# Stage-1 units one place later, and one matrix load behind a transposing transfer

## The chip, the cores and the metric

One of the eight cores of a Trainium2 chip runs the program. The metric is the device time of one execution in microseconds. The median of three runs of the kernel before is 1419.41 us (1419.1 to 1424.3). Times inside the program come from one further execution that the hardware profiler recorded; they count from the first instruction of its span.

## The reference

Block-causal attention, then a gated layer pair, then a mixture of experts with a greedy assignment of tokens:

```
scores = (q @ k^T) / sqrt(64); mask by blocks of 64; attn = softmax(scores)
x   = attn @ v                              # 8 batches x 8 heads x 576 x 64 -> 4608 x 512
x   = ((x @ w1) * (x @ w2)) @ w3 @ w_out     # 512 -> 1024 -> 1024 -> 512
logits = x @ w_gate                         # 8 experts
assign each token to an expert, pairs (token, expert) in falling order of logit, 576 tokens each
out[tokens of e] = relu(x @ ew1[e]) @ ew2[e]
```

Everything is kept exact enough by splitting operands into a high and a low half in a narrow type; a product is then three matmuls.

## The kernel before

**Stage 1** works in half steps h = 0 to 63, two for each pair of heads, eight for each batch b. A half step makes score tiles on TensorE (`s_tiles`, lines 331 to 395), their exponentials on ScalarE (357), sums, scaled high and low halves on VectorE and ScalarE (P, 371 to 377), a transposing DMA of P on SP's queue (416, `PT`), and some half steps later the product with v (`pv`, 434), whose result is read out by ScalarE (445) and VectorE (440) into `xT[b]`. `xT[b]` holds all 512 features of a batch's 576 tokens.

Between them run the **units** of `moe_unit`: 128 of them, 16 for each batch. Unit u takes half of a batch's tokens (288) and one of eight column blocks of w1 and w2: 12 matmuls for w1 and 12 for w2 (line 467), a read-out by ScalarE (`a_sb`, 477), the product on VectorE (`g`, 483), and, every second unit, a write of `g` to DRAM on SP's queue (485). The eight units of the first token half of batch b need four finished `pv` of that batch, those of the second half all eight. Smaller products follow the units: `logits` (521), and `turn` (542 to 546), which brings the routing logits into the tile `L` by way of ScalarE's copies `lgT` (529).

The order is a list of events by place: `at(p, f)` puts f at place p, counted in half steps, and events run in the order of p. On TensorE this order is binding in stage 1 (`manual_schedule` with PE alone); on the other engines a scheduler orders the instructions. The units' places are `slots`: two in each half step, at .26 and at .6. The units of batch 0 take the first 16 slots; from unit 16 on two slots are skipped. Events after h = 64 (units, logits, loads for the next stage) form a tail without attention work; it closes with `run(70.2)` and the logits of the last 16 units.

**Stage 2** routes: seven phases of short VectorE and TensorE steps that depend on one another. It starts from `L`. The waits of TensorE in it are filled with the matmuls `px` (1161), which compute the 36 blocks of 128 rows of x; each block is written to `xr` in DRAM by SP's queue (1218), the last one by SP (1212) for the 512 values and by ScalarE's queue (1214, `sq`) for a sum of squares for each row, 128 values of 4 bytes.

**Stage 3** computes the experts. `gather(p)` fetches 128 rows of `xr` at a time by an indirect DMA from GpSimd's queue (1340), splits them (`x16`, 1344 and 1345) and turns them: the first block on TensorE (1350, read out at 1353 and 1355 as `xT`), all others by a transposing DMA on SP's queue (1360). `layer1` (1387) and `layer2` (1405) follow. For the first expert, layer 1 runs over token blocks: eight products for the first 128 tokens, eight for the second, eight for the third, eight for the last 192, which reach over the fourth and fifth block. The experts' matrices are 2048 KB each and come by SP's queue (1249, `esa` and `esb`) into a buffer of one; `behind_row` puts such a load behind the transfer kept in `last_row[0]` in SP's order. The load of expert 2's first matrix is the first one that `phase_of` issues this way; its values are first read in the third of the calls of `phase_of`.

Of the kernel before, what the change touches and what calls it, by code (L numbers as in the profile page):

```python
# [56 lines left out]
def moe_kernel(ctx, tc, q, k, v, moe_w1, moe_w2, moe_w3, moe_w_out, w_gate, ew1, ew2, out):  # L57
    nc = tc.nc
    P = 128
# [16 lines left out]
    def pow2(pool, m, name, TB=TB, **kw):  # L76
        n = m.shape[-1]
        t = pool.tile([P, 3, n], I32, name=name, **kw)
        nc.vector.tensor_scalar(t[:, 0], m.bitcast(I32), 24, 23, op0=ALU.logical_shift_right,
                                op1=ALU.logical_shift_left)  # L80
        nc.vector.tensor_scalar(t[:, 1], t[:, 0], -1.0, float((189 + TB) << 23), op0=ALU.mult, op1=ALU.add)
        nc.vector.tensor_scalar(t[:, 2], t[:, 0], float((65 - TB) << 23), None, op0=ALU.add)
        return t[:, 1].bitcast(F32), t[:, 2].bitcast(F32)
# [33 lines left out]
    def at(p, f, *a):  # L117
        assert p >= now[0], (p, now[0])
        heapq.heappush(ev, (p, at.n, f, a))
        at.n += 1  # L120
# [6 lines left out]
    def run(end):  # L127
        while ev and ev[0][0] < end:
            now[0], _, f, a = heapq.heappop(ev)
            f(*a)  # L130
# [381 lines left out]
    def logits(u):  # L512
        b, r = divmod(u, 16)
        half, f = divmod(r, 8)
        if f == 0:
            hold("l")
            lg["ps"] = ps_ab.tile([P, 512], F32, name="ab")
        p = lg["ps"]
        gh = lg.pop(u) if u >= UL else lt[u // 8][:, u % 8]
        r = 32 * (f % 4)  # L520
        nc.tensor.matmul(p[r:r + 32, :288], W34g[:, f, :], gh, start=f < 4, stop=f >= 4)
        if f < 7:
            return
        odd = b % 2

        def rows_out():
            if half == 0:
                lgT[0] = mo.tile([P, S], F32, name="lgT", bufs=1)
            nc.scalar.activation(lgT[0][:, half * 288:half * 288 + 288], p[:, :288], AF.Copy)
            if half == 1 and not odd:  # L530
                lgT[1] = mo.tile([P, 64], F32, name="lgx", bufs=2)
                nc.scalar.activation(lgT[1], p[:, 224:288], AF.Copy)
            held.remove("l")
            if half == 1:
                defer(.1, alone, "l", turn)

        def turn():
            hold("l")
            t, n = lgT[0], 4 + odd
            p = ps_ab.tile([P, 512], F32, name="ab")  # L540
            if odd:
                nc.tensor.matmul(p[:64, :8], lgT[1], i8, start=True, stop=True)
                nc.tensor.matmul(p[64:, :8], t[:, :64], i8, start=True, stop=True)
            for j in range(odd, n):
                c = j * P - 64 * odd
                lg["o"] = nc.tensor.matmul(p[:, j * 8:j * 8 + 8], t[:, c:c + P], i8, start=True, stop=True)
            jb = 9 * (b // 2) + 4 * odd

            def keep():
                nc.vector.tensor_copy(L[:, jb:jb + n, :], p[:, :n * 8].rearrange("p (j e) -> p j e", e=8))  # L550
                held.remove("l")

            defer(.06, keep)

        defer(.1, rows_out)
# [229 lines left out]
    def pair(h):  # L785
        b, r = divmod(h, 8)
        return 4 * b + r % 4, int(r < 4)
# [17 lines left out]
        at(h, tiles, h)  # L805
    for h in range(2 * NS):
        at(h + 1.35 if h + 1 < HS else h + 2.93, alone, "v", pv, *pair(h))
    slots = [h + x for h in range(5, 73) for x in (.26, .6)]
    for u in range(128):
        at(slots[u if u < 16 else u + 2], moe_unit, u)  # L810
    for n in range(NS):
        b, r = divmod(n, 4)
        at(8 * b + r + (.85 if b < 2 else 1.7), prep_v, n)
# [365 lines left out]
    def prep_g(j, d=0):  # L1179
        load_g(j)  # L1180
        split_g(j, d)
# [42 lines left out]
    def fill(n):  # L1224
        owed[0] += n
        while owed[0] >= 1:
            owed[0] -= 1
            next(st_, None)
# [7 lines left out]
    early, last_row = {}, [None]  # L1236
# [47 lines left out]
    at(67.9, prep_g, 0, 1.0)  # L1284
    at(68.3, prep_g, 1, 1.0)
    with tc.manual_schedule(engines=MS):
        run(70.2)
        for u in range(UL, 126):
            logits(u)
            if u % 8 == 7:  # L1290
                run(now[0] + .5)
        fill(16)
        for u in range(126, 128):
            logits(u)
        run(100)
        prep_g(2)
# [34 lines left out]
    xT2, scs, hs, scat = {}, {}, {}, []  # L1331

    def gather(p):
        def block(h):
            if h == 0:
                xT2[p] = ce.tile([P, 8, NG * P], F16, name="xT2")
                scs[p] = ce.tile([P, NG], F32, name="sc")
            xg = ce.tile([P, DM + 1], F32, name="xg", bufs=4)
            c = p * NG + h
            nc.gpsimd.indirect_dma_start(out=xg, out_offset=None, in_=xr,  # L1340
                                         in_offset=bass.IndirectOffsetOnAxis(ap=idx[:, c:c + 1], axis=0))
            x16 = ce.tile([P, 2, DM], F16, name="x16", bufs=4)
            s, i = pow2(ce, xg[:, DM:], "xsc", TBX, bufs=4)
            nc.scalar.activation(x16[:, 0], xg[:, :DM], AF.Copy, scale=s)  # L1344
            nc.vector.scalar_tensor_tensor(x16[:, 1], xg[:, :DM], s, x16[:, 0], op0=ALU.mult, op1=ALU.subtract)  # L1345
            def by_pe():
                for z in range(2):
                    t = pe_.tile([P, 512], F32, name="pe")
                    for c_ in range(4):
                        nc.tensor.matmul(t[:, c_ * P:c_ * P + P], x16[:, z, c_ * P:c_ * P + P], id16, start=True, stop=True)  # L1350
                    dst, src_ = xT2[p][:, 4 * z:4 * z + 4, :P], t.rearrange("p (c t) -> p c t", c=4)
                    if z:
                        nc.vector.tensor_copy(dst, src_)
                    else:
                        nc.scalar.activation(dst, src_, AF.Copy)  # L1355

            if p == 0 and h == 0:
                owed_.append(by_pe)
            else:
                nc.sync.dma_start_transpose(out=xT2[p][:, :, h * P:h * P + P], in_=x16.rearrange("p z d -> p (z d)"))  # L1360
            nc.vector.tensor_copy(scs[p][:, h:h + 1], i)
            if p == 0 and h == 1:
                owed_.pop()()

        return [lambda h=h: block(h) for h in range(NG)]

    def layer1(e, parts):
# [108 lines left out]
```

## Time and profile before

| | us |
|---|---|
| median of three runs | 1419.41 |
| the profiled execution | 1424.65 |
| its span, first to last instruction | 1422.9 |
| TensorE busy in the span | 1312.7 (92%) |
| VectorE, ScalarE busy | 962.9 (68%), 952.5 (67%) |
| mean granted TensorE clock | 0.98 |

Stage 1 ends at about 763 us, stage 2 at about 1020 us, and stage 3 fills the rest. The page shows busy time by engine, the tables by stretch show it by stage with the granted clock of TensorE (1.00 is 2.4 GHz, 0.50 is 1.2 GHz) and the share of the DMA engines that is busy, and the timelines show what ended an engine's idle time.

### The profile page before, as it was taken

The numbers are of one execution on the slowest core, as the hardware profiler recorded it, in microseconds if no ns is written. First come the engines' busy times: TensorE is split into PE (matmuls) and PEld (weight loads), VectorE is DVE, ScalarE is ACT, GpSimd is POOL, SyncE is SP. The second block draws the span as 40 slices with busy tenths as digits, with TensorE's granted clock in tenths as the row PEclk, the third lists the DMA queues.
The fourth block names the chain that finished last, engine by engine and source line by source line (L and its number), as shares of the span: only waits on it lengthen the run. The fifth ranks groups of instructions, "written<-read, shape, count | busy, mean of one in ns | idle before, by whom it ended". The sixth has DMA issues, their size and how long they took to land. (4 is left out here: it accounts for less than half of the span.)

```text
span 1422.9 us, 31992 instructions
## 1 busy us (share of the span) xinstructions
PE 1312.7 (92%) x12487; PEld 905.1 (64%) x12487; DVE 962.9 (68%) x2873; ACT 952.5 (67%) x2229; POOL 115.1 (8%) x141
## 2 busy tenths in 40 slices
PE   4669789988999989999999999999899999999997
PEld 2446567666766757666776666666786566655663
DVE  7988878887988878887414777777455456454530
ACT  7897887978889877877534555554247667675641
POOL 0000000000000000010011111110122221120001
PEclk9899999999999999999999999999999999999999
DMA  9877978797878778799998998879576676654200
GB/s 294 199 182 197 211 154 182 139 213 192 182 192 194 168 181 166 151 207 233 239 291 184 253 229 210 200 189 215 154 144 160 161 197 161 163 172 138 82 23 37
DMA packets 384150, 257.45 MB, mean 181 GB/s; under 512 B 261120, under 2 KB 345088, under 8 KB 382976
## 3 DMA queue, kind: packets, MB, share of 16 engines
q1 hardware_dynamic: 370656, 213.44, 61.2%
q0 software_dynamic: 11520, 39.87, 12.6%
q10 hardware_dynamic: 1824, 2.11, 0.5%
q8 instruction: 97, 1.59, 0.5%
q14 instruction: 53, 0.43, 0.1%
HBM read 130.84 MB, written 39.86 MB: 120 GB/s over the span
## 5 line engine op out<-in xcount | busy, mean ns | idle before, releaser
L467 PE MATMUL ab<-xT,w1h 128*128 128x288 f16 x1536 | 217.4, 291 | 11.9 <-DVE xT L440 4.0
L467 PE MATMUL ab<-xT,w2h 128*128 128x288 f16 x1536 | 212.5, 288 | 4.3 <-ACT a_sb L477 2.9
L1387 PE MATMUL pe<-xT,ewa 128*128 128x288 f16 (+2 forms) x1728 | 192.1, 275 | 1.7 <-ACT xT L1355 1.0
L467 PEld LDWEIGHTS <-w1h 128*128 128x128 f16 x1536 | 145.9, 99 | 71.1 <-issue 29.0
L1405 PE MATMUL pe<-ewb,h 128*128 128x512 f16 (+1 forms) x960 | 188.5, 379 | 0.0
L467 PEld LDWEIGHTS <-w2h 128*128 128x128 f16 x1536 | 151.0, 99 | 47.0 <-issue 7.0
L1387 PEld LDWEIGHTS <-ewa 128*128 128x128 f16 x1728 | 157.0, 99 | 36.3 <-issue 2.0
L377 DVE SCALAR_TENSOR_TENSOR P<-E,rr,P 128x128 f16<-128x128 f32 (+4 forms) x288 | 157.3, 583 | 25.8 <-ACT P L373 25.4
L357 ACT ACTIVATE E<-S,nb,cc 128x384 f32<-128x384 f32 (+4 forms) x234 | 147.7, 640 | 1.9
L1405 PEld LDWEIGHTS <-h 128*128 128x128 f16 (+1 forms) x960 | 84.8, 100 | 99.7 <-issue 2.6
L373 ACT ACTIVATE P<-E,rr 128x384 f16<-128x384 f32 (+2 forms) x224 | 120.5, 603 | 17.0 <-issue 5.4
L1161 PE MATMUL px<-W34h,gh 128*128 128x512 f32 x288 | 120.0, 417 | 0.0
L1161 PE MATMUL px<-W34h,gl 128*128 128x512 f32 x288 | 119.5, 415 | 0.3 <-DMA gl<-g 0.3
L1161 PE MATMUL px<-W34l,gh 128*128 128x512 f32 x288 | 119.8, 416 | 0.0
L434 PE MATMUL PV<-PT,v 128*64 128x128 f16 (+1 forms) x2880 | 89.7, 219 | 18.8 <-DMA PT<-P 17.3
L349 DVE TENSOR_REDUCE nb<-S 128x2 f32<-128x768 f32 (+3 forms) x128 | 100.7, 817 | 4.2 <-PE S L335 3.9
L434 PEld LDWEIGHTS <-v 128*64 128x64 f16 x2880 | 78.8, 115 | 38.7 <-issue 28.3
L1390 DVE SCALAR_TENSOR_TENSOR h<-pe,h 128x288 f16<-128x288 f32 (+2 forms) x144 | 57.8, 420 | 45.9 <-ACT h L1389 44.5
L1408 ACT ACTIVATE y<-pe,s 128x512 f32<-128x512 f32 x36 | 24.7, 687 | 94.8 <-PE pe L1405 59.6
L1345 DVE SCALAR_TENSOR_TENSOR x<-xg,xsc,x 128x512 f16<-128x512 f32 x36 | 27.1, 752 | 84.1 <-ACT x L1344 84.1
L1216 ACT ACTIVATE jk<-px 128x512 f16<-128x512 f32 x35 | 20.9, 596 | 94.1 <-issue 84.3
L1389 ACT ACTIVATE h<-pe 128x288 f16<-128x288 f32 (+2 forms) x144 | 52.5, 376 | 43.4 <-PE pe L1387 37.5
(301 smaller groups left out, 2263.7 us busy)
## 6 DMA issues: line engine op xcount, KB each, us to landing
g<-gd SPq DMA_DIRECT2D x36, 512.0 KB, 4.2
gl<-g POOLq DMA_DIRECT2D x36, 512.0 KB
raw<-in_moe_w_dram SPq DMA_DIRECT2D x32, 512.0 KB, 3.4
gd<-g SPq DMA_DIRECT2D x56, 288.0 KB, 3.0
g<-gd SPq DMA_DIRECT2D x14, 1152.0 KB, 8.7
esa<-in_moe_w_dram SPq DMA_DIRECT2D x6, 2048.0 KB
esb<-in_moe_w_dram SPq DMA_DIRECT2D x6, 2048.0 KB, 8.7
v<-in_v_dram SPq DMA_DIRECT2D x8, 1280.0 KB, 7.7
```

The lines of the kernel that those rows point to most:

```text
L349: newest["m"] = nc.vector.tensor_reduce(nb[:, 0, x:x + 2], ps[:, :, o:o + N], axis=AX.X, op=ALU.max)
L357: newest["e"] = nc.scalar.activation(d["e"][:, cols[x]], pf_[:, cols[x]], AF.Exp, bias=nb[:, 1, x:x + 1], scale=c[:, 0:1], accum_out=sums[ ...
L373: nc.scalar.activation(hi, d["e"][:, cols[x]], AF.Copy, scale=r[:, 1, x:x + 1])
L377: nc.vector.scalar_tensor_tensor(lo, d["e"][:, cols[x]], r[:, 1, x:x + 1], hi, op0=ALU.mult, op1=ALU.subtract)
L434: nc.tensor.matmul(ps[hh * 64:hh * 64 + 64, c0:c0 + w], vt[:, zv, hh, j, :], s, start=z == 0 and j == 0, stop=z == 2 and j == nj - 1)
L467: nc.tensor.matmul(p[:, :288], w[:, zw, cc, :], x[:, zx, cc, c0:c0 + 288], start=first, stop=cc == 3 and zw == 1)
L1161: nc.tensor.matmul(p, gh[a][:, f], W34[b][:, f], start=f == 0 and a + b == 0, stop=f == 7 and a == 1)
L1345: nc.vector.scalar_tensor_tensor(x16[:, 1], xg[:, :DM], s, x16[:, 0], op0=ALU.mult, op1=ALU.subtract)
L1387: nc.tensor.matmul(p[:, :n], w1[:, a, cc, f * P:(f + 1) * P], t[:, 4 * b + cc, x], start=cc == 0 and a + b == 0, stop=cc == 3 and a == 1)
L1389: nc.scalar.activation(h[:, 0, f, x], p[:, :n], AF.Relu)
L1390: nc.vector.scalar_tensor_tensor(h[:, 1, f, x], p[:, :n], 0.0, h[:, 0, f, x], op0=ALU.max, op1=ALU.subtract)
L1405: nc.tensor.matmul(p[r0:r1], h[:, a, f, k_ * P + r0:k_ * P + r1], EW[e, "b"][0][:, b, f], start=f == 0 and a + b == 0, stop=f == 7 and a == 1)
```

## The change

```diff
-    slots = [h + x for h in range(5, 73) for x in (.26, .6)]
+    slots = [h + x for h in range(5, 74) for x in (.26, .6)]
     for u in range(128):
-        at(slots[u if u < 16 else u + 2], moe_unit, u)
+        at(slots[u if u < 16 else u + 3], moe_unit, u)
...
-        run(70.2)
+        run(70.7)
...
             else:
-                nc.sync.dma_start_transpose(out=xT2[p][:, :, h * P:h * P + P], in_=x16.rearrange("p z d -> p (z d)"))
+                d = nc.sync.dma_start_transpose(out=xT2[p][:, :, h * P:h * P + P], in_=x16.rearrange("p z d -> p (z d)"))
+                if p == 0 and h == 1:
+                    last_row[0] = d
```

No computation, tile or transfer is added or taken away. Units 16 to 127 move on by one slot: a unit that stood at .26 now stands at .6 of the same half step, one that stood at .6 at .26 of the next. On TensorE each place from 14.6 to 69.6 therefore still holds one unit, the one before; place 14.26 is empty and place 70.26 is new. In the tail, 72 matmuls of line 467 in a row become 96; after the first matmul of the last `turn` 19 matmuls `px` follow ahead of its other three, where 24 stood.

ScalarE at half step 14, where `a_sb` are reads of units, `junk` the squares of q and k that a small product on TensorE (line 147) waits for, `v` squares of v and `P` a high half. Before:

```order
L204 ACTIVATE v_2279,vm<-v_122 128x1024
L477 ACTIVATE a_sb<-ab 128x288
L373 ACTIVATE P_120<-E,rr 128x576
L204 ACTIVATE junk,qm<-qk_2112 128x1152
L204 ACTIVATE wo_2525,wom<-wo_2523 128x512
L577 ACTIVATE dec<-raw 128x512
L204 ACTIVATE v_2279,vm<-v_122 128x512
L355 ACTIVATE nb<-nb,cc 128x2
```

and now:

```order
L204 ACTIVATE v_2250,vm<-v_122 128x1024
L355 ACTIVATE nb<-nb,cc 128x2
L204 ACTIVATE junk,qm<-qk_2112 128x1152
L355 ACTIVATE nb<-nb,cc 128x1
L373 ACTIVATE P_120<-E,rr 128x576
L204 ACTIVATE v_2250,vm<-v_122 128x512
```

The read of the unit is gone from this place, and the squares stand ahead of the high half `P`, behind a small `nb` that needs VectorE's maxima of a score tile.

ScalarE at the end of the tail, where `gl` and `gh` prepare the operands of `px` from loads `g` of SP's queue, and the two `lgT` belong to the two last halves of the logits. Before:

```order
L477 ACTIVATE a_sb<-ab 128x288
L1191 ACTIVATE gh<-g_12232 128x1024
L1191 ACTIVATE gh<-g_12266 128x1024
L529 ACTIVATE lgT<-ab 128x288
L1188 ACTIVATE gl<-g_12442 128x1024
L1191 ACTIVATE gh<-g_12442 128x1024
L529 ACTIVATE lgT<-ab 128x288
```

and now:

```order
L477 ACTIVATE a_sb<-ab 128x288
L1191 ACTIVATE gh<-g_12203 128x1024
L477 ACTIVATE a_sb<-ab 128x288
L1191 ACTIVATE gh<-g_12235 128x1024
L529 ACTIVATE lgT<-ab 128x288
L1188 ACTIVATE gl<-g_12442 128x1024
L1191 ACTIVATE gh<-g_12442 128x1024
L529 ACTIVATE lgT<-ab 128x288
```

One more read of a unit stands there; the last `lgT` is still behind the third `gl` and `gh`.

SP's queue between the stages 2 and 3. Before:

```order
L1218 DMA xr<-row 128x513 x4
L1212 DMA xr<-row 128x512
L1249 DMA esa<-in_moe_w_dram 128x4x1024
L1360 DMA_TRANSPOSE xT_16584<-x_16598 128x8x128
L1360 DMA_TRANSPOSE xT_16584<-x_16638 128x8x128
```

and now:

```order
L1218 DMA xr<-row 128x513 x4
L1212 DMA xr<-row 128x512
L1360 DMA_TRANSPOSE xT_16584<-x_16598 128x8x128
L1249 DMA esa<-in_moe_w_dram 128x4x1024
L1360 DMA_TRANSPOSE xT_16584<-x_16638 128x8x128
```

The load of 2048 KB has moved from ahead of the first transposing transfer to behind it, and ahead of the second.

## Rows read from the trace of the kernel before

**Rows 1.** Busy time by stretch: length, each engine's us (instructions), clock, DMA share, GB/s.

```profile
164.00:176.00 12.00, 6.76 (x97) 4.56 (x96) 8.30 (x18) 10.03 (x23) 0.00 (x0) 0.99 0.97 256
...
420.00:560.00 140.00, 131.57 (x1629) 93.83 (x1628) 118.26 (x307) 118.37 (x287) 0.00 (x0) 0.99 0.82 183
...
675.00:763.00 88.00, 87.44 (x946) 63.12 (x946) 24.58 (x52) 38.91 (x78) 6.08 (x7) 1.00 0.99 247
```

**Rows 2.** Waits of TensorE, 160 to 760 us: total us, times, longest.

```profile
PE ab L147 <- ACT junk L204: 8.9, 3, 4.9
...
PE ab L467 <- DVE xT L440: 4.0, 5, 1.9
...
PE ab L467 <- ACT xT L445: 0.7, 1, 0.7
```

**Rows 3.** Timeline of TensorE, stage 1: start, length, work, idle before and releaser.

```profile
175.66 0.16 PE L147 MATMUL ab<-qm,ones 128*128 128x2 bf16 x1 [4.86 <-ACT junk L204]
...
500.30 0.41 PE L467 MATMUL ab<-xT,w1h 128*128 128x288 f16 x2 [1.92 <-DVE xT L440]
...
530.25 2.17 PE L467 MATMUL ab<-xT,w1h 128*128 128x288 f16 x10 [2.26 <-DVE g L483]
```

**Rows 4.** Timeline of TensorE, end of the tail of stage 1.

```profile
746.72 1.63 PE L467 MATMUL ab<-xT,w1h 128*128 128x288 f16 x12
...
749.75 2.13 PE L521 MATMUL ab<-gq,W34g 128*32 128x288 f32 x28
...
755.66 0.68 PE L521 MATMUL ab<-gq,W34g 128*32 128x288 f32 x4
...
763.38 0.84 PE L546 MATMUL ab<-i,lgT 128*128 128x8 f32 x6 [0.94 <-ACT lgT L529]
```

**Rows 5.** Timeline of ScalarE, end of the tail.

```profile
761.02 1.06 ACT L1188 ACTIVATE gl<-g 128x1024 fp32r<-128x1024 f32 x1 [9.56 <-DMA g<-gd]
...
762.93 0.39 ACT L529 ACTIVATE lgT<-ab 128x288 f32<-128x288 f32 x1
```

**Rows 6.** Timeline of SP's queue: end of the tail, and stage 3.

```profile
755.35 0.36 SPq L1177 DMA_DIRECT2D g<-gd  x1
...
1019.93 0.43 SPq L1249 DMA_DIRECT2D esa<-in_moe_w_dram  x1
...
1045.07 1.23 SPq L1360 DMA_TRANSPOSE xT<-x  x1
```

**Rows 7.** The chain that ended last: start, length, what; from stage 2 to 3.

```profile
1020.34 6.30 DMA xr<-sq
...
1035.51 25.88 PE pe L1387 x383
```

**Rows 8.** DMA issues: KB each, median us to landing; the last from 1034 to 1062 us.

```profile
esb<-in_moe_w_dram SPq DMA_DIRECT2D x6, 2048.0 KB, 8.7
...
xr<-row SPq DMA_DIRECT2D x1, 256.0 KB, 3.0
...
xT<-x SPq DMA_TRANSPOSE x8, 6.2
```

**Rows 9.** DMA queues, 1019 to 1024 us, then 1024 to 1028: packets, MB, engines' share.

```profile
q1 hardware_dynamic: 292, 0.87, 70.4%
...
q1 hardware_dynamic: 377, 1.49, 90.7%
q10 hardware_dynamic: 144, 0.00, 2.0%
```

**Rows 10.** Busy time by stretch, start of stage 3.

```profile
1032.40:1039.20 6.80, 4.72 (x44) 4.24 (x41) 3.49 (x14) 2.37 (x5) 1.91 (x3) 0.50 0.78 185
1036.00:1047.00 11.00, 11.00 (x171) 11.00 (x170) 6.02 (x30) 5.31 (x16) 2.84 (x4) 0.85 0.81 156
```

**Rows 11.** Timeline of ScalarE: reads of layer 1's products, third and last token group.

```profile
1053.51 0.28 ACT L1389 ACTIVATE h<-pe 128x128 f16<-128x128 f32 x1 [0.39 <-PE pe L1387]
1054.50 0.33 ACT L1389 ACTIVATE h<-pe 128x192 f16<-128x192 f32 x1 [0.71 <-PE pe L1387]
```

## The prediction, made before the changed kernel ran

> **What bounds the kernel now.** I read the busy time by stretch first, because the two edits lie in different stages. In the tail of stage 1 TensorE works without a break, 87.4 of 88.0 us; in the attention part it works 131.6 of 140 us; around half step 14 only 6.8 of 12 us [rows 1]. So a matmul costs nothing at half step 14 and its full time in the tail. Then the waits of TensorE in stage 1 [rows 2]: two kinds matter. One is the wait for the squares of q and k (8.9 us in three, 4.9 of it at 175.66 us, the middle of half step 14) [rows 2, 3]. The other is the wait of a unit for `xT`, 4.0 us in five waits for VectorE and 0.7 in one for ScalarE [rows 2], the longest 1.92 us at 500.30 [rows 3]. Last the chain between the stages 2 and 3. It holds 6.30 us in which the transfer of 512 bytes from `sq` is under way, and only behind it come the gathers, and the dense run of layer 1 from 1035.51 us [rows 7]. From there to the end TensorE hardly waits, so what that start gains, the end gains.
>
> **Edit 1, units one slot later.** Three things change.
>
> (a) The waits for `xT`. A batch's first unit of either token half stands at 6.26 or 10.26 of its batch, a third of a half step behind the last `pv` that it needs (places 5.93 and 9.93). Now another unit stands between. A unit takes 749.75 - 746.72 = 3.03 us [rows 4], more than the longest wait of 1.92 us [rows 3], so all of these waits should go: 4.0 + 0.7 = 4.7 us [rows 2]. What is late next are ScalarE and VectorE themselves: 30 us behind the 1.92 us stands a wait of 2.26 us for a unit's `g` [rows 3], and with VectorE at 118 and ScalarE at 118 of 140 us [rows 1] I can't tell whether these two move forward with TensorE or keep their time and take the gain back. The bounds are 0 and 4.7 us; I take half, 2.4.
>
> (b) The unit that leaves place 14.26 frees 3.03 us of TensorE ahead of 175.66, where TensorE then waits for the squares. Only what comes forward on ScalarE counts: a read of a unit (0.4 us by its neighbours of the same size, such as the 0.39 us of `lgT` [rows 5]) no longer stands there and the second squares stand ahead of a high half. Against this stands the small `nb`, which waits for VectorE. The bounds are a loss of 0.4 (the squares as late behind `nb` as they were early behind the unit) and a gain of 3.03; nearest is the work that leaves ScalarE's queue ahead of the squares, a read and a high half of some 0.7. I take 0.9.
>
> (c) The same unit comes back at 70.26, where TensorE has no gap [rows 1]. Uncovered it costs 3.03. But stage 2 starts from the last `turn`, and there TensorE waited 0.94 us for `lgT` [rows 4]. That copy ran at 762.93 although its logits had ended at 756.34 (755.66 + 0.68) [rows 4], since ScalarE, in order, first waited 9.56 us for the load of the third `g`, issued at 755.35 [rows 5, 6]. This load hangs on transfers of earlier tiles, not on the last unit, and keeps its time. So the unit is covered by the wait of 0.94, and by the five `px` that now stand behind the `turn` instead of ahead of it. 24 of them lie between 756.34 and 762.44 (763.38 - 0.94), 0.25 us each, so five are 1.25. What is left is 3.03 - 0.94 - 1.25 = 0.8 us. If that cover is gone, it is 3.03.
>
> Edit 1 together: -2.4 - 0.9 + 0.8 = -2.5 us.
>
> **Edit 2, the load behind the first transposing transfer.** Before, SP issues 2048 KB at 1019.93 [rows 6], 0.41 us ahead of `sq` [rows 7]. In 1019 to 1024 us the DMA engines carry packets of SP's queue alone; those of `sq` (128, with 16 for the semaphore) all fall into 1024 to 1028, between 90.7% of the load [rows 9]. The row block written just ahead lands in 3.0 us though it is 500 times larger [rows 8]. Now nothing of that size is under way. `sq` needs at most the 3.0 us of a whole row block, which saves 3.3. At best the gathers wait for that row block alone (issued just ahead of the load, landed at 1022.6), which saves 4.1. I take 3.7 us: the gathers, and with them the dense run, start that much earlier.
>
> The Trainium skill ("DMA: Bandwidth & Descriptors", section on queues, rings and completion order) says that each DMA engine takes turns between queues packet by packet. By that rule `sq`, on a queue of its own, would hardly have waited for the load, and its 6.30 us would be its own; the sum would then have 0 in place of 3.7. The trace shows its packets starting late rather than moving slowly [rows 9], and I follow the trace.
>
> What the load is put in front of is the price. All transposing transfers but the first are now behind it on SP's queue. The fourth was issued at 1045.07 [rows 6] and took some 6.2 us [rows 8], so it landed near 1051.3. It is needed by the last token group, whose first product is read at 1054.50 and took 1.0 (the distance to the read before) [rows 11]: needed near 1053.4, a margin of 2.1 us. The load takes 90.7% x 4 us / 1.49 MB x 2.1 MB = 5.1 us of all engines [rows 9]; of the 11 us around it the engines were busy 81% [rows 10], which leaves 2.1 us to take it up. So TensorE waits 5.1 - 2.1 - 2.1 = 0.9 us, take 1.0; with nothing to take it up 3.0; with the engines really free 0. Of the transfers for this expert the fourth is the last one issued, and I take it as the one that decides. The load's own reader comes two calls of `phase_of` later and isn't touched.
>
> The clock: TensorE idled ahead of the dense run and then got 0.50 from 1032.40 to 1039.20 [rows 10]. Of this the 3.7 us behind 1035.51 were dense and lost half, 1.85 us. The idle time gets shorter, but the steps from gather to first product still leave TensorE nearly idle. I leave the 1.85 as it is and keep it as an upside.
>
> Edit 2 together: -3.7 + 1.0 = -2.7 us.
>
> **Sum.** -2.5 - 2.7 = -5.2. Against the profiled execution, 1424.65 us, that is 1419.45. This execution was 5.2 us above the median of the runs, 1419.41; one of the three runs (1424.3) is as high, so executions differ by this much without any change. I apply the difference to the median: **1414.2 us**.
>
> **The rivals.**
> - *All of it comes through.* The attention part follows TensorE: (a) 4.7, (b) 3.03, (c) still 0.8 lost; edit 2 saves 4.1 with no wait for the transposing transfers, and the clock stays up, 1.85. That is 4.7 + 3.03 - 0.8 + 4.1 + 1.85 = 12.9 us, 1406.5. For it: TensorE is the busiest engine over most of the stretch. Against: VectorE and ScalarE are at 84% there [rows 1].
> - *The unit comes back uncovered.* The waits for `xT` are replaced by waits for ScalarE and VectorE, half step 14 gives nothing, and the load of `g` slides with the units: +3.03 - 2.7 = +0.3, 1419.7. For it: the unit goes from where TensorE has 5 us to spare to where it has 0.6 [rows 1].
> - *Slower: the transposing transfers wait out the whole load.* A load of this size takes 8.7 us to land [rows 8]. If all of it comes ahead of the fourth block, TensorE waits 8.7 - 2.1 = 6.6 us, loses the clock for another 6.8 us at half speed (3.4), and with edit 1's 2.5 the sum is -2.5 - 3.7 + 6.6 + 3.4 = +3.8: 1423.2. This decides from the point where the load costs the transposing more than 2.1 + 3.7 = 5.8 us. Against it: the engines have gaps there [rows 10].
> - *`sq` is slow by itself*, as the rule above would have it. Edit 2 then saves nothing and costs 1.0: -2.5 + 1.0 = -1.5, 1417.9.
>
> That the change doesn't do what it says is excluded by the order of the instructions.
>
> **How the numbers follow.** Chances: the forecast 0.42, all of it 0.22, the uncovered unit 0.15, the waiting transfers 0.09, the slow `sq` 0.12. A measurement of this kernel can tell about 0.5% from no change, 7.1 us, so 1412.3 and 1426.5 are the borders. Faster is nearly all of the second case (0.20) and the better third of the forecast's own range of 1409 to 1418 (0.14): 0.34. Slower is the upper part of the waiting transfers, where half of their case passes 1426.5 as some executions are 5 us higher, 0.05, and 0.01 of the rest: 0.06. Same is 0.60. The range leaves out a tenth on either side: 1405.5 to 1422.5.
>
> **What the profile will show.** Right: no wait of line 467 for `xT`; the last `turn` near 1 us later than its place in the tail, still behind the third `gl`; `xr<-sq` in the chain with 2.2 to 3.0 us; the dense run of layer 1 starting 3.7 us sooner against the end of stage 2; a wait of about 1 us for a transposing transfer ahead of the last token group. Wrong: new waits of line 467 for `a_sb` or `g` as large as those for `xT`; `sq` still above 5 us; a wait above 4 us in the first expert's layer 1.

## The result, and the profile after

| | us |
|---|---|
| kernel before, median of 6 runs | 1419.8 (1419.1 to 1424.3) |
| changed kernel, median of 6 runs | 1428.44 (1428.2 to 1430.02) |
| ratio, 95% interval | 1.0055, 1.0041 to 1.0069 |
| profiled execution of the changed kernel; its span | 1428.2; 1426.1 |
| both once more on another chip: 28 and 12 runs | 1421.36 and 1426.52, ratio 1.0038, 1.0019 to 1.0057 |

The change made the kernel slower, by 8.6 us in the first comparison and by 5.2 in the second; the intervals overlap between 1.0041 and 1.0057, which is 6 to 8 us. I had forecast 1414.2 us and a range that ended at 1422.5.

The profile after answers to the rows of before. First the waits of TensorE from 160 to 760 us (what waited, for what; total us, times, longest):

```profile
PE ab L467 <- ACT a_sb L477: 12.7, 11, 3.3
PE ab L147 <- ACT junk L204: 8.3, 2, 5.3
...
PE ab L467 <- DVE g L483: 3.7, 3, 2.3
```

The waits of units for `xT`, 4.7 us before [rows 2], are gone. Waits for the read-out `a_sb` stand in their place: 12.7 us, against 5.0 before (the row "PE ab L467 <- ACT a_sb L477: 5.0, 8, 1.0" of the same view of before), and the longest is 3.3 instead of 1.0.

The timeline of TensorE (start, length, work, idle before and its releaser) shows where:

```profile
172.95 0.16 PE L147 MATMUL ab<-qm,ones 128*128 128x2 bf16 x1 [5.27 <-ACT junk L204]
...
182.67 2.28 PE L467 MATMUL ab<-xT,w2h 128*128 128x288 f16 x12 [3.33 <-ACT a_sb L477]
...
193.05 1.63 PE L467 MATMUL ab<-xT,w1h 128*128 128x288 f16 x12 [1.37 <-ACT a_sb L477]
```

The squares end the first wait at 172.95 instead of 175.66 [rows 3], so they did come forward. Ten us later a unit waits 3.33 us for ScalarE.

The chain that ended last, between the stages 2 and 3:

```profile
1018.71 2.28 DMA xr<-sq
...
1033.57 15.04 DMA xT<-x
1048.60 0.05 issue
1048.65 13.38 PE pe L1389 x161
```

`sq` now lands in 2.28 us instead of 6.30 [rows 7]. But the second transposing transfer, issued at 1033.57, lands 15.04 us later, and layer 1 (line 1389 here) waits for it. The timeline of TensorE and the granted clock from 1047.10 to 1053.90 us (columns as in [rows 1]) show the cost:

```profile
1029.87 12.45 PE L1389 MATMUL pe<-xT,ewa 128*128 128x128 f16 x191 [0.57 <-DVE xT L1353]
1048.65 15.94 PE L1389 MATMUL pe<-xT,ewa 128*128 128x128 f16 x192 [6.33 <-DMA xT<-x]
```

```profile
1047.10:1053.90 6.80, 5.25 (x50) 5.26 (x51) 1.87 (x6) 1.72 (x5) 0.94 (x1) 0.50 1.13 133
```

The dense run starts at 1029.87, 5.64 us sooner than in [rows 7]; 1.6 us of this lie ahead of the end of the last `px`. In the middle of it TensorE waits 6.33 us, and the first 5.25 us of matmuls behind that get 0.50 of the clock (1.2 GHz). Before, there was no such wait.

### The profile page after: what moved, and what is told of

Same layout as the page of the kernel before. It is cut to its first block, busy times and chain, and to the rows that moved or that the text cites. A ratio compares the mean times of both kernels' runs of the same rounds, so it can differ in the third digit from the quotient of the medians.

```text
span 1426.1 us, 31998 instructions
## 1 busy us (share of the span) xinstructions
PE 1309.8 (92%) x12487; PEld 905.4 (63%) x12487; DVE 963.5 (68%) x2873; ACT 952.1 (67%) x2229; POOL 114.9 (8%) x141
## 5 line engine op out<-in xcount | busy, mean ns | idle before, releaser
L467 PE MATMUL ab<-xT,w1h 128*128 128x288 f16 x1536 | 214.0, 290 | 10.5 <-ACT a_sb L477 5.3
L467 PE MATMUL ab<-xT,w2h 128*128 128x288 f16 x1536 | 211.6, 288 | 12.3 <-ACT a_sb L477 7.7
L467 PEld LDWEIGHTS <-w1h 128*128 128x128 f16 x1536 | 145.4, 99 | 66.9 <-issue 25.2
L467 PEld LDWEIGHTS <-w2h 128*128 128x128 f16 x1536 | 150.4, 98 | 54.7 <-issue 15.5
```

Of the source, the lines that this page charges most:

```text
L467: nc.tensor.matmul(p[:, :288], w[:, zw, cc, :], x[:, zx, cc, c0:c0 + 288], start=first, stop=cc == 3 and zw == 1)
```

## The experiments

All times are medians against the kernel before on the same chip, whose medians were 1420.78 to 1421.39 us (28 to 35 runs each). The ratios are estimates from all runs and can differ from the quotient of two medians by up to 0.16%. "Base" is the kernel with the old unit table and the load behind the eighth transposing transfer.

### The kernel before again, and each edit alone

The kernel before, unchanged:

> The kernel before once more, for a second profile and the spread of its time. Both theories: 1419 to 1424 us, the first layer's dense run starting near 1035.5 us and running without a wait of 4 us or more.

Measured: 1423.22 us, ratio 0.9999 (0.9981 to 1.0017). Its profiled execution was one of the short ones, 1417.25 us. The waits fit the first profile of before:

```profile
PE ab L467 <- ACT a_sb L477: 5.5, 8, 1.0
PE ab L467 <- DVE xT L440: 4.0, 5, 1.9
```

Here and below, half step h of a trace is the stretch from the first matmul of the product with v (`pv`) of half step h-1 to that of half step h. That product stands at place h + 2.93 (h + 1.35 before half step 13), so in this count the place 14.26 and the wait for the squares both lie in half step 13.

The half steps 9 to 26 took 195.4 us here and 201.0 in the profile that I predicted from. From half step 27 to 45 both have the same lengths to 0.1 us. So one execution differs from the next by some 5 us inside stage 1, and a loss of that size can't be read from one profile of each kernel: in the first pair the markers of stage 1 agreed from half step 47 on to 0.1 us, and I took the units for harmless. The times of many runs are needed, and the waits, which repeat.

The units alone, twice:

```diff
-    slots = [h + x for h in range(5, 73) for x in (.26, .6)]
+    slots = [h + x for h in range(5, 74) for x in (.26, .6)]
-        at(slots[u if u < 16 else u + 2], moe_unit, u)
+        at(slots[u if u < 16 else u + 3], moe_unit, u)
-        run(70.2)
+        run(70.7)
```

> The unit table alone is changed; the load stands where it stood. Theory (the load behind the first transposing transfer is the cause): the markers of stage 1 end 0 to 0.7 us later than before, the wait for sq's read stays at 6 us, so 1420 to 1421 us. Rival (the units' new place costs the time, by later a_sb, g and w3r): 1424 to 1428 us.

> The new unit table alone, once more. Theory: 1.0025 to 1.0035 of before, 1424.5 to 1426 us. Rival (its first result was high): under 1.0015, 1423 us or less.

Measured: 1425.98 us, 1.0031 (1.0011 to 1.0051), and 1426.31 us, 1.0036 (1.0021 to 1.0050). This is the rival of the first expectation; the second result lies just above its own range. The unit table alone costs 4.6 to 5 us; the intervals reach 2.1 to 2.8 us either way.

The load alone, twice:

```diff
-                nc.sync.dma_start_transpose(out=xT2[p][:, :, h * P:h * P + P], ...
+                d = nc.sync.dma_start_transpose(out=xT2[p][:, :, h * P:h * P + P], ...
+                if p == 0 and h == 1:
+                    last_row[0] = d
```

> The load behind the first transposing transfer alone; the unit table is as before. Theory: sq's read falls from 6.3 to about 2.3 us (-4.0), PE then waits 6.3 us for the second transposing transfer and runs the columns behind it at the lower clock for another 2 to 3 us, sum about +5: 1424 to 1428 us. Rival (units): at most 1420 us.

> The load behind the first transposing transfer with the old unit table, once more. Theory (sq -4.2, first layer +8.0): +3 to +4.5 against the kernel before, 1424 to 1426 us, and +8 against the base of this group. Rival, by its first result (1.0002 of before): 1421 to 1422.5 us; the base is then 6 us under it.

Measured: 1422.68 us, 1.0002 (0.9982 to 1.0022), and 1420.72 us, 1.0000 (0.9980 to 1.0019). The theory, that the load is the cause of the loss, falls: its times, 1424 us and more, were missed twice. The rivals were missed as well, the first (at most 1420) from above and the second (1421 to 1422.5) by 0.3 us from below. In the two profiles, the first and then the second, the same program waits for the same transfer for 6.25 us in one and 2.84 in the other.

```profile
1044.81 14.69 PE L1389 MATMUL pe<-xT,ewa 128*128 128x128 f16 x192 [6.25 <-DMA xT<-x]
```

```profile
1039.42 5.53 PE L1389 MATMUL pe<-xT,ewa 128*128 128x128 f16 x96 [2.84 <-DMA xT<-x]
```

From the start of the dense run to the last matmul it takes 386.3 and 382.4 us, where the kernels with the load at its old place take 378.3 to 378.8: a loss of 8.0 and 4.0. The gain at `sq` is the same in both: from the last `px` to the dense run 12.0 and 12.3 us instead of 16.2 to 16.8, so 4.2. The sum is +3.8 or -0.2; the timed runs say about 0, give or take 2.8. How often an execution is of either kind isn't shown.

The changed kernel again, measured beside the units alone:

> The changed kernel once more, beside the units alone. Theory (the load's move is worth 0 to +1 by itself, and the same with the new table): within 1.5 us of the units alone, 1425 to 1427 us, 1.003 to 1.004 of before. Rival (the edits hurt each other): 3 us or more over the units alone, 1428 to 1430 us.

The edit is the whole change. Measured: 1426.52 us, 1.0038 (1.0019 to 1.0057), 0.2 over the units alone. So in this comparison the loss is the unit table's; the load's move is neither a gain nor a loss that these runs can tell. Its profile waits 6.22 us for the transfer, as the first profile of the changed kernel does.

### Where the load may stand

The same edit with `h == 8` in place of `h == 1`, three times:

> The load behind the eighth, the last transposing transfer, the unit table as before. Theory: sq's read 2.3 us, transposing transfers land 1 to 2 us apart, no wait of 6 us in the first layer's dense run; -4 to -6, so 1414 to 1416 us. Rival (what is won at sq is given back anyway, at the clock or at layer 2's own loads, which then come later): 1419 to 1420 us; if the matrix of the second layer now lands after its first reader asks for it, a wait for esa shows at that layer's start.

> The load behind the eighth transposing transfer with the old unit table, once more, as the base of this group. Theory: 1414 to 1417 us, 4 to 6 us under the kernel before. Rival (its first result was chance): 1418 us or more.

> The load behind the eighth with the old unit table: the base for the next run. Both: 1414 to 1417 us.

Measured: 1415.48, 1414.98 and 1416.16 us; 0.9942 (0.9919 to 0.9964), 0.9963 (0.9946 to 0.9979), 0.9963 (0.9948 to 0.9978). This version beats both kernels, by 5 to 6 us the one before. Of the second profile, the chain and then the timeline of TensorE:

```profile
1014.57 2.13 DMA xr<-sq
```

```profile
1025.75 25.73 PE L1389 MATMUL pe<-xT,ewa 128*128 128x128 f16 x383 [0.56 <-DVE xT L1353]
1051.32 1.89 PE L1407 MATMUL pe<-ewb,h 128*128 128x512 f16 x8
```

`sq` lands as fast as in the changed kernel, and layer 1 runs its 383 matmuls through, 25.73 us as before [rows 7]. Layer 2 starts behind it without a wait. The load is not missed later either: from the first product of layer 1 to the last matmul it takes 378.5 us, as with the load at its old place (378.3 to 378.8).

Behind the fourth (`h == 4`):

> The old table, the load behind the fourth transposing transfer. Theory (a transposing transfer behind the load lands some 15 us after its issue; the fifth to the eighth are read from the third token group on): blocks one to four land as before, block five about 15 us after its issue at 1045 to 1047 us, PE waits 4 to 8 us for it: 1418 to 1422 us. Rival (only the first few reads of the layer are in a hurry): no wait of over 1 us, 1414 to 1417 us.

Measured: 1417.31 us, 0.9975 (0.9965 to 0.9986). The rival holds, with a time 0.3 us above its range: layer 1 has no wait for a transfer. The fifth block's transfer took long in this run too (the longest of the stretch 13.8 us, from the rows of the tile), but nobody needed it sooner. What counts is that the load stands behind the transfers that are read in a hurry; that it matters how far behind, these runs don't show.

The load at the changed kernel's time, but on ScalarE's own queue:

```diff
-                nc.sync.dma_start(d["st"], src[e].rearrange(...))
+                (nc.scalar if part == 0 and e == 2 else nc.sync).dma_start(d["st"], src[e].rearrange(...))
...
         for f in blocks[:2]:
             f()
+        mats[4][0]()
+        mats[4] = (lambda: None), mats[4][1]
```

> The old unit table; the load at the time of the changed kernel, behind the first transposing transfer, but issued by ScalarE on its own queue. Theory (a transposing transfer waits for what stands ahead of it on its own queue): the second lands 5 to 8 us after its issue, PE waits for it under 1.5 us, 1415 to 1418 us. Rival (the DMA engines are full while 2 MB move, whatever queue they stand on): it lands 12 us or more after its issue, PE waits 4 to 7 us, 1421 to 1425 us.

Measured: 1426.0 us, 1.0033 (1.0019 to 1.0047). The rival holds, and more than that. ScalarE issued the load just ahead of the first transposing transfer. The timeline of ScalarE's queue, the chain, and the DMA issues from 1024 to 1042 us (median us to landing, here from the one landing of each row that the trace holds):

```profile
1024.51 0.39 ACTq L1249 DMA_DIRECT2D esa<-in_moe_w_dram  x1
```

```profile
1025.21 15.63 DMA xT<-x
```

```profile
xg<-xr,idx POOLq DMA_INDIRECT x5, 10.7
xT<-x SPq DMA_TRANSPOSE x4, 13.6
```

Now the very first transposing transfer takes 15.63 us, on a queue without the load, and TensorE waits 7.9 us for it. A gather, on a third queue, lands in 10.7 us (median 4.4 in the base over 1020 to 1080 us). So it doesn't take the order within a queue to make the transfers wait. The load takes the DMA engines from all queues: from 1026 to 1034 us ScalarE's queue moves 2.08 MB in 79.6% of the engines' time, SP's queue 0.10 MB. The Trainium skill ("DMA: Bandwidth & Descriptors", section "Issuing engines are not separate DMA queues") says this: transfers of all issuing engines run on the same 16 DMA engines and interleave there, so issuing from several saves only issue time. The 15.63 us here, against 11.64 to 15.43 on one queue, agree with it.

This is about half of the time only. The transfer lands at 1040.84, some 7 us after the load is through, and from 1034 to 1041 us SP's queue takes 93.6% of the engines' time for 0.38 MB. In the second profile of the kernel before, 0.52 MB of such transfers took 50.6% of 6 us (1032 to 1038), a third of the engines' time for each MB. The changed kernel's trace has the same two parts, the load from 1034 to 1041 us and slow small packets to 1048.6. What slows them behind the load isn't shown.

### Which units cost

The new table with the load behind the eighth:

> The new unit table together with the load behind the eighth transposing transfer. Theory (the two edits are separate costs that add up: table +4.4, load at its new place +4, sq -4.2): against the kernel with the old table and the load behind the eighth, +3 to +4.5, so 1418 to 1421 us; half step 40 lasts 18.0 us instead of 16.3. Rival (the table costs nothing once the load is well placed, its +4.4 being chance): 1414 to 1416 us.

Measured: 1419.25 us, 0.9990 (0.9974 to 1.0006). That is 3.6 us over the next run, on the same chip, in which only eight units are moved. So the table costs 3.6 us with the load well placed and 4.6 to 5 with the load at its old place: the theory of a cost of its own holds. Half step 40, though, lasted 16.3 us, not the 18.0 of the theory.

Units 76 to 83 alone, with the load behind the eighth:

```diff
-        at(slots[u if u < 16 else u + 2], moe_unit, u)
+        at(slots[u if u < 16 else u + 3 if 76 <= u < 84 else u + 2], moe_unit, u)
```

> The load behind the eighth; of the units only 76 to 83 one place later, the eight before the wait of 1.9 us for xT in half step 44. Theory: half step 40 stays at 16.3 us, half step 44 falls from 16.7 to 15.7 us and this is kept to the end of stage 1, -1.0 against the kernel with the old table: 1413 to 1416 us. Rival (the wait is only moved, to w34o, w3r or g): 16.7 us over half steps 44 to 47 are given back, change 0.

Measured: 1415.67 us, 0.9965 (0.9953 to 0.9978), no better than the base. The rival holds. Half step 44 fell from 16.70 to 14.99 us, but half steps 42 and 43 took 18.55 instead of 16.94, and half steps 40 to 63 together are 266.25 us, in the base's three profiles 266.0 to 266.2. The wait for `xT` became a new one of 1.9 us for `a_sb`.

Units 64 and later alone (`u + 2 if u < 64 else u + 3`), the load at its old place:

> The load where it stood; of the units only 64 and later one place later, so that the early half steps (up to 37) keep their order. Theory (the table costs in two places, +1.7 net at half steps 40 to 47 and at the tail, and +2 or more before half step 26): the late part alone +1 to +2.5, 1421 to 1424 us; half step 40 at 18.0 us, half step 44 at 15.7 us. Rival (all of the cost is late): +4, 1425 us. Rival (all of it early): 1420 to 1421.5 us.

Measured: 1422.82 us, 1.0013 (1.0001 to 1.0026), the time that the theory had, but by another route. The cut leaves place 38.26 empty, which is in half step 36. That half step got 2.9 us shorter, half step 38 3.5 us longer, and in the latter the trace shows

```profile
438.55 2.46 PE L467 MATMUL ab<-xT,w1h 128*128 128x288 f16 x12 [2.06 <-ACT a_sb L477]
```

Half step 40 lasts 16.7 us, not 18.0; half step 44 lasts 15.7, as expected.

Units 16 to 63 alone (`u + 3 if u < 64 else u + 2`), with the load behind the eighth; then the same with the shift tapering off between units 48 and 64, so that no two share a place:

> The load behind the eighth; of the units only 16 to 63 one place later, 64 and later where they were (63 and 64 then share a place). Theory (of the table's +3.6 to +4.4, the late part was +1.5, so the rest is early): +2 to +3 against the base, 1417 to 1419 us, with half steps 38 and 40 as in the base. Rival (the early part costs nothing, the halves only cost together): within 0.7 us of the base.

> The load behind the eighth; units 16 to 48 one place later, the shift tapering off to none at unit 64, so that no two share a place and units 64 and later stand where they stood. Theory (the early half costs +2, in the half steps before 26): +1.5 to +3 against the base, 1416.5 to 1418.5 us, half step 36 at 9.7 us again. Rival (early half free, the loss of the first such run was the shared place and the routing): within 1 us of the base.

Measured: 1421.74 us (1.0006, 0.9993 to 1.0019) and 1421.47 us (1.0004, 0.9994 to 1.0014), 6.8 and 5.3 over the base on the same chip. Neither the theories nor the rivals hold. Part of the loss is a unit's own work: the unit that leaves place 14.26 comes back here within the attention part. Half step 36 of the first and half step 32 of the second hold 72 matmuls of line 467 instead of 48, and they last 2.6 and 3.0 us longer (12.23 instead of 9.68, 11.47 instead of 8.43), where a unit takes 3.03 [rows 4]. In the whole new table this unit stands in the tail. By difference 4.2 and 2.3 us are left for the early part, but the traces don't settle it: up to half step 31 the two take 253.6 and 253.5 us from the `pv` of half step 8, the base's three profiles 251.3 to 253.0. So the size of the early part stays open.

### The loss in the trace

What repeats in every profile of the new table and in none of the old is a wait of 2.3 to 3.5 us for `a_sb` in half step 13; the longest wait for `a_sb` is 1.0 in the nine profiles with the whole old table. ScalarE's timeline, of the units alone:

```profile
176.87 1.18 ACT L204 ACTIVATE junk<-qk 128x1152 f16<-128x1152 f32 x1
177.92 0.22 ACT L204 ACTIVATION_READ_ACCUMULATOR junk<-qk 128x1 bf16 x1
178.01 2.41 ACT L190 ACTIVATE qkT<-qk,qp 128x1152 f16<-128x1152 f32 x2
180.31 1.07 ACT L204 ACTIVATE v<-v 128x1024 f16<-128x1024 f32 x1
181.25 0.22 ACT L204 ACTIVATION_READ_ACCUMULATOR v<-v 128x1 bf16 x1
181.34 0.42 ACT L477 ACTIVATE a_sb<-ab 128x288 f32<-128x288 f32 x1
```

TensorE had ended the w1 products of a second unit near 178.3 and then waited 3.47 us, to 181.81, for this read of the unit ahead of it, whose product was ready near 175.1. The read stood behind the squares, two scalings `qkT` and the squares of v. In the second profile of the base a read runs at 176.91, ahead of that block.

The lengths of the stretches in us (mean over profiles, standard deviation; the ten are those nine and that of units 76 to 83 alone):

| stretch | old table, 10 profiles | new table, 5 profiles |
|---|---|---|
| half steps 9 to 15 | 87.9 (0.9) | 87.9 (1.4) |
| 16 to 26 | 109.9 (1.1) | 111.3 (0.5) |
| 27 to 39 | 135.4 (0.0) | 135.5 (0.3) |
| 40 to 63 | 266.4 (0.5) | 266.6 (0.9) |
| tail, to the first step of stage 2 | 49.6 (0.2) | 50.3 (0.1) |

Together +2.5 us, of which the tail's 0.7 and the 1.4 of half steps 16 to 26 stand out of the spread. Half steps 9 to 15 hold one unit less than before and are no shorter.

The waits add up to nearly the same. Over half steps 9 to 63 those of TensorE are 39.4 us in the mean of the nine profiles (38.1 to 40.8) and 44.2 in the five (43.2 to 45.9), 4.8 more: the waits for `xT` fall by 4.8, those for `a_sb` rise from 5.7 to 12.1, and those for `PT`, `g`, `w34o` and `w3h` by 1.3 to 1.8 each; two waits ahead of score tiles fall by 1.3 and 1.4. The work in this stretch falls by 2.8 us, as a unit moves to the tail, where it costs 0.7. That is 4.8 - 2.8 + 0.7 = 2.7 us.

The timed loss of 3.6 to 5 us is larger. Part of the rest may be the clock: its mean over the timed runs was 0.9735 and 0.9732 for the kernel before, 0.9707 and 0.9700 for the units alone on the same chips. Which stretches lose it wasn't settled.

One place can be shown. In half step 40 the new order takes away two waits for `xT`, 1.1 us together, and the products of `wo` then wait for VectorE's `w3h`, 2.0 us instead of 0.7. The same row of the changed kernel in its first profile and in its second:

```profile
459.96 6.60 PE L726 MATMUL ab<-wo,w3h 128*128 128x512 f16 x22 [2.01 <-DVE w3h L185]
```

```profile
460.13 4.92 PE L726 MATMUL ab<-wo,w3h 128*128 128x512 f16 x22 [2.02 <-DVE w3h L185]
```

The wait is the same; in the first the 22 matmuls behind it took 1.7 us more. The granted clock from 458.5 to 465 us was 0.74 in the first, a mean of its two levels, and 1.00 in the second; for the units alone it was likewise 0.74 in their first profile and 1.00 (458 to 464 us) in their second. So this wait cost its own length or nearly twice that.

## Why the prediction was wrong

- **(a) The waits for `xT`, -2.4.** They went, all 4.7 us of them, as said. The gain did not stay: in the first pair of profiles the waits for `a_sb` rose from 5.0 to 12.7 us and those for `g` from 2.3 to 3.7. I had written that I could not tell whether ScalarE and VectorE "keep their time and take the gain back", and bounded that case at 0. That bound is the step that failed first: the waits of TensorE did not shrink by 0 to 4.7 us, they grew by 4.8 over half steps 9 to 63. A moved unit does not only find its input later or sooner; its read-out gets another place in ScalarE's queue, and that can cost more than the wait was worth. The run of units 76 to 83 shows the exchange at its plainest: 1.7 us won, 1.6 lost.
- **(b) Half step 14, -0.9.** The squares came forward, as the mechanism had it: the wait for them ends 56.1 us behind the `pv` of half step 8 in the mean of the five profiles, 57.4 in the ten of the old table. I counted what leaves ScalarE's queue ahead of them, and not what then stands behind them: the read of the next unit, queued behind 4.5 us of squares and scalings (176.87 to 181.34), made TensorE wait 2.3 to 3.5 us. The gain is spent by half step 15 (87.9 us either way).
- **(c) The tail, +0.8.** Measured +0.7, with a small spread. The cover (the wait for `lgT`, and five `px`) held: the last `turn` runs at 764.09 us without a wait, 0.7 us later than in [rows 4].
- **Edit 1 together** was put at -2.5 and measured +3.6 to +5.0. Sign and size are wrong.
- **`sq`, -3.7.** Measured 2.0 to 2.5 us for the transfer wherever the chain shows it with the load placed later, and 4.2 us from the last `px` to the dense run. Right, slightly over my upper bound of 4.1. The rival of a `sq` that is slow by itself is refuted.
- **The transposing transfers, +1.0.** This is the second step that failed: 4 to 9 us in the four profiles. I took the fourth transfer as the one that decides, with a margin of 2.1 us, and let the engines' idle 19% take up 2.1 us of the load. It was the second one, read at the 193rd matmul, with the load directly in front of it. The rival of the transfers that wait out the load had the mechanism and, with 6.6 us of waiting and 3.4 of clock, nearly the price (6.3, and 2.5 for the matmuls behind it up to the end); I gave it 0.09. Its transfer was the wrong one as well.
- **The clock.** The 1.85 us were not an upside: behind the new wait the clock was at 0.50 again.
- **Edit 2 together** was put at -2.7 and measured 0.0 (1.0000 and 1.0002); -2.7 lies at the edge of both intervals.
- **The reference point.** I left the 5.2 us between the profiled execution and the median unexplained. Half steps 9 to 26, the very part from which (b) was read, took 201.0 us in it, 3.2 more than in the mean of the ten profiles and 5.6 more than in the shorter execution; the rest isn't located.

The sum of the measured parts, +5 for the units and 0 for the load, gives the +5.2 of the second comparison. The first gave 8.6. In both profiles of the changed kernel the load loses 9.1 us behind the start of layer 1 and gains 4.2 ahead of it, and with the units' 3.6 to 5 that would be 8.5 to 9.9; whether the six runs of the first comparison were all of this kind isn't shown. Both intervals allow 6 to 8.

## What to carry to other kernels

Before a step is moved on one engine, look up where its read-out then stands in the other engines' queues: waits of 4.8 us for an input were paid here with 6.3 us more for the read-out, which had come to stand behind other work in ScalarE's queue. A large load is to be put behind the small transfers that are read in a hurry, and the transfer to look at is the first one behind the load, not the last one issued; another queue didn't help here. Where two executions of one program differ by as much as the change, compare waits that repeat and medians, not markers of a single pair.

## What was not expected of the hardware

- The first transposing transfer behind a load of 2 MB landed after 11.6 to 15.6 us, on the load's queue and on another one alike, against 4.3 to 6.1 in the second profile of the kernel before. In the changed kernel about 7 of the 15.04 us lie behind the load's last packets. SP was held too: the issue of one such transfer took up to 6.30 us with the load on SP's queue and 5.20 with it on ScalarE's, against 1.23 [rows 6].
- The same wait of 2.0 us was followed by 1.7 us of lost clock in two of five executions and by none in three.
- The 512 bytes of `sq`, on ScalarE's queue, took 6.3 to 6.9 us with that load just issued on SP's, and 2.0 to 2.5 us without. The Trainium skill's rule of engines that take turns between queues packet by packet ("DMA: Bandwidth & Descriptors", section on queues, rings and completion order) would have let it through; the trace doesn't show that.
